# Retention and a bilinear FFN on one core: the last output product in two halves on two PSUM banks, and two products of h moved from GpSimd to VectorE

## Chip, core and metric

The kernel runs on one core of one Trainium2 chip. The metric is the device time of a run in microseconds (us). Times of the profile are those of one profiled execution of the same program.

## What is computed

A retention recurrence feeds a feed-forward block whose two input products are multiplied elementwise. Inputs and output are float32; products run in bfloat16 with float32 sums.

```
q, k, v: [4, 8, 768, 64]; w_a, w_b: [512, 1536]; w_out: [1536, 512]
state_t = gamma_h * state_{t-1} + k_t^T v_t        # per batch and head
y_t     = (1/8) * q_t state_t
x       = y, heads side by side: [3072, 512]
out     = ((x @ w_a) * (x @ w_b)) @ w_out          # [3072, 512]
```

## The kernel before, in words

The 3072 tokens are cut into 24 tiles of 128, in seven blocks `J` of 4, 2, 2, 2, 2, 4 and 8 tiles. Retention, the casts of weights and inputs, and the feed-forward blocks of earlier tokens are interleaved by hand: a helper `seq` chains every instruction to the one before it on its engine, so the order on each engine is the order of the text. Tiles come from pools with a fixed number of buffers; a new tile waits until the last reader of the buffer that it gets is done.

The last block (`BIG`, J = 6, 1024 tokens) is a stage of its own, run by `big()`. It replaces eight block products by seven with sums around them, twice.

The products with `w_a` and `w_b` are done by twelve units `u0` to `u11`. Unit `u` has a pair number `p = u // 2` and one of the weights, `a` for even and `b` for odd units. Its seven products (methods p1 to p7) go into three PSUM banks: "A" from a ring of three banks (`psff`), "B" from two fixed banks, one for the even and one for the odd units (`uB`), and "C". Each product is two matmuls of 512 columns. Bank A is built up in steps, and ScalarE copies it out after a step (`snap`, line 795). `Unit.leave` (line 797) adds a copy and a bank on VectorE: for an `a` unit into a tile `asb` (pool of 5 buffers), for a `b` unit into `gsb` (pool of 6). Behind a `gsb` stands the product of h = gsb * asb, 128x512 in bf16, on GpSimd for the pairs 0 to 4 and on VectorE for the last pair. That product is also the last reader of its `gsb` and `asb`. GpSimd works through sums of weights (`weight_pieces`, tiles `wsa` and `wsb`) in between.

The products with `w_out` are done by four groups `a`, `b`, `c`, `d` of 256 tokens (class `Group`), again seven products of 6 matmuls of 256 columns each, in banks `mA`, `mB`, `mC`. ScalarE copies bank A after steps 1, 6 and 5 into `snaps[:, 0]` to `snaps[:, 2]` (line 657). VectorE adds a copy to bank B or C into an output row tile `osb` (pool of 6 buffers), ScalarE copies bank A after the last step (p3), and `leave` (line 669) issues the output on SyncE's queue (SP).

The two orders `START` and `END` are written out by hand. The program closes with `c7 d7 c6 d6 S14 c5 d5 c3 c4 d4 d3`. So `d3`, the step p3 of group d, is the last product: six matmuls add S4 times the lower right quarter of `w_out` (`B22`) to bank A, ScalarE copies the 128x256 result (line 700), and two DMAs, one on ScalarE's queue and one on SP's, each send the rows of 64 partitions (line 702). Step `d4` stands directly ahead of it, with its own add on VectorE and its own output DMA on SP.

Of the kernel before, what the change touches and what calls it, by code (L numbers as in the profile page):

```python
# [9 lines left out]
F32 = mybir.dt.float32  # L10
BF16 = mybir.dt.bfloat16
AF = mybir.ActivationFunctionType
ALU = mybir.AluOpType
# [16 lines left out]
def kernel(  # L30
# [10 lines left out]
    nc = tc.nc  # L41
    P = 128
# [26 lines left out]
    osbp = ctx.enter_context(tc.tile_pool(name="osbp", bufs=6))  # L69
# [25 lines left out]
    psff = Ring()  # L95
# [4 lines left out]
    def seq(bi):  # L100
        ins = bi.ins
        prev = last.get(ins.engine)
        if prev is not None:
            tc.add_manual_dep(ins, prev.name, nosync, reason="program order")
        last[ins.engine] = ins
        return bi
# [125 lines left out]
    NP = NFT // 2  # L232
    DH = DM // 2
    wsum = wpool.tile([P, 3, NP, DH], BF16, name="wsum")
    wo_v = wo_bf.rearrange("p (two j) (c d) -> p two c j d", two=2, c=2)
    B11, B12, B21, B22 = (wo_v[:, k2, c] for k2 in range(2) for c in range(2))
    T2, T3, T4 = (wsum[:, n] for n in range(3))
    BIG = len(TILES) - 1
# [86 lines left out]
    def half(i):  # L325
        return slice(64 * i, 64 * i + 64)
# [63 lines left out]
    def leave(t):  # L390
        J, i = where[t]
        key, i = (J, i) if J < BIG else ((J, i // 4), i % 4)
        if i == 0:
            pool, tag = (wstage, "w") if key == (BIG, 1) else (xtp, "xt")
            xt[key] = pool.tile([P, KT, 4 * P], BF16, tag=tag, name="xt")
        for r in range(2):
            seq(nc.scalar.copy(xt[key][:, 2 * r : 2 * r + 2, i * P : (i + 2) * P],
                               ys[t // 2][r].rearrange("p j a s n -> p j (a s n)")))

    def turn(new, old, eng=nc.scalar):  # L400
        if old is not None:
            ys[old // 2] = [psat.tile([P, 2, 2, 2, P // 2], F32, tag=f"y{r}", name="y") for r in range(2)]
        two = new is not None and (new + 1) % NCH < NCH - 1
        if new is not None:
            if two or old is None:
                update(new, eng)
            scores(new + 1, "y" if old is None else "ff")
            scores(new, "at")
        if old is not None:
            inter(old)  # L410
            inter(old + 1)
        if two:
            update(new + 1, nc.scalar)
        elif new is not None and old is not None:
            update(new, eng)
        if old is not None:
            intra(old)
            intra(old + 1)
            leave(old)
# [158 lines left out]
    def rows(J, u, r):  # L578
        n0 = (sum(TILES[:J]) + 2 * u) * P
        return out[n0 : n0 + 2 * P, :].rearrange("(n r) d -> r n d", r=2)[r]  # L580

    def tt(dst, x, y, op, eng=nc.vector):
        seq(eng.tensor_tensor(dst, x, y, op=op))  # L583
# [13 lines left out]
    hs = {}  # L597
# [30 lines left out]
    class Group:  # L628
# [66 lines left out]
                self.leave(1, DH, DM)  # L695

        def p3(self):
            self.product("A", 4, B22, False)
            if self.J == BIG and self.i == 3:
                seq(nc.scalar.copy(self.row(0)[:, DH:], self.bank["A"]))  # L700
                for n, queue in enumerate((nc.scalar, nc.sync)):
                    seq(queue.dma_start(out=rows(self.J, self.i, 0)[half(n), DH:],
                                        in_=self.osb[0][half(n), DH:]))
                return
            seq(nc.scalar.copy(self.row(0)[:, DH:], self.bank["A"]))
            psff.back(self.whole["A"])
            self.leave(0)

        def p4(self):
            self.product("B", (1, 1), T4, False)  # L710
            tt(self.row(1)[:, :DH], self.bank["B"], self.snaps[:, 1], ALU.add)
            psff.back(self.whole["B"])
            self.leave(1, 0, DH if self.J == BIG and self.i > 1 else DM)
# [31 lines left out]
    def weight_pieces(n):  # L745
        for _ in range(min(n, len(pieces))):
            weight_piece(*pieces.pop(0))
# [16 lines left out]
    def h_big(c):  # L764
        if (BIG, c) not in ht:
            ht[BIG, c] = htp.tile([P, NFT, 4 * P], BF16, tag="ht", name="ht")
        return ht[BIG, c]

    class Unit:
# [27 lines left out]
        def leave(self, i, c, bank, n):  # L797
            if self.w == "a":
                dst = half_a[self.p, i, c] = asbp.tile([P, 4 * P], BF16, tag="asb", name="asb")
                tt(dst, self.bank[bank], self.snaps[n], ALU.add)  # L800
                return
            g = nat.tile([P, 4 * P], BF16, tag="vb", name="gsb")
            tt(g, self.bank[bank], self.snaps[n], ALU.add)
            tt(h_big(c)[:, NP * i + self.p], g, half_a.pop((self.p, i, c)), ALU.mult,
               nc.gpsimd if self.p < NP - 1 else nc.vector)
            weight_pieces(2 if self.p < 2 else 1)

        def p1(self):
# [270 lines left out]
```

## Time and profile before

| what | value |
|---|---|
| median of 3 runs | 221.32 us (220.12 to 221.72) |
| the profiled execution | 220.11 us |
| its span from first to last instruction | 218.4 us (218.402) |
| granted TensorE clock | 0.999 |
| TensorE busy | 211.5 us, 97% of the span |
| GpSimd busy | 150.0 us, 69% |
| VectorE busy | 139.5 us, 64% |
| ScalarE busy | 100.9 us, 46% |

In the lines of the profile, PE is TensorE's matmul, PEld its weight load, DVE VectorE, ACT ScalarE, POOL GpSimd, SPq and ACTq the DMA issues on the queues of SyncE and ScalarE. L583 is line 583 of the kernel, here a helper `tt` that all two-input adds and products go through, so tiles tell them apart and not the line. A timeline row has the start in us, the length, engine, line, operation, output<-inputs with partitions x elements and types, and a count; in brackets stands the engine's idle time ahead of it and who ended it. The length of a row with several matmuls runs to the end of the last, which overlaps the next one's start.

### The profile page before, as it was taken

The page shows a single profiled execution, that of the slowest core. Times are in us where ns is not written, and L with a number is a line of the kernel's source. Part 1 is how long each engine was busy: PE and PEld are TensorE (multiplying, and loading weights), DVE is VectorE, ACT ScalarE, POOL GpSimd, SP SyncE. Part 2 cuts the span into 40 slices and gives each one's busy share as a digit, 9 for nine tenths or more (in the row PEclk, how much of TensorE's full clock was granted, in tenths as well). Part 3 has the DMA queues.
Part 4 walks back from the last instruction along what each step waited for, and adds up shares of the span by engine and source line. Part 5 has one row for each costly group of instructions (what it writes and reads, how often), then busy time and mean ns, then how long its engine had stood idle before and what let it go on. Part 6 is the DMA issues. An engine that isn't in the chain of part 4 may idle for free.

```text
span 218.4 us, 5659 instructions
## 1 busy us (share of the span) xinstructions
PE 211.5 (97%) x2238; PEld 143.5 (66%) x2238; DVE 139.5 (64%) x255; ACT 100.9 (46%) x221; POOL 150.0 (69%) x174
## 2 busy tenths in 40 slices
PE   7889999999999999999999999999999999999993
PEld 3557445687458888888888655457864444458882
DVE  3776346845883485455477246876678676788961
ACT  3256335343234445464576245456545665652430
POOL 5265876878444578569847949989999999970000
PEclk9999999999999999999999999999999999999999
DMA  6999999999999999999999999970022000000145
GB/s 164 290 322 366 384 310 358 384 253 240 183 255 246 200 230 217 194 218 245 211 177 254 209 209 230 246 80 5 3 88 104 0 2 3 0 2 0 36 183 168
DMA packets 85018, 39.68 MB, mean 182 GB/s; under 512 B 57472, under 2 KB 78720, under 8 KB 84992
## 3 DMA queue, kind: packets, MB, share of 16 engines
q1 hardware_dynamic: 84912, 39.26, 79.8%
q8 instruction: 17, 0.28, 0.6%
q10 hardware_dynamic: 80, 0.07, 0.1%
q14 instruction: 9, 0.07, 0.1%
HBM read 28.31 MB, written 6.29 MB: 158 GB/s over the span
## 4 chain that ended last, share of the span: by engine, by line
PE 89%; SPq 4%; DMA 4%; POOL 0%; issue 0%; ACT 0%
PE g L545 19%; PE a L533 19%; PE mA L650 12%; PE uA L788 9%; PE mB L650 6%; PE uB L788 5%; PE o L570 5%; DMA wstb<-in_moe_w_b_dram 4%; SPq L132 3%; PE mC L650 3%; PE at L338 2%; PE uC L788 2%; PE y L386 2%; PE st L356 2%; PE y L376 1%; SPq L152 1%
## 5 line engine op out<-in xcount | busy, mean ns | idle before, releaser
L547 DVE TENSOR_TENSOR ht<-g,asb 128x256 bf16<-128x256 f32 (+1 forms) x74 | 37.2, 503 | 37.8 <-PE g L545 34.4
L533 PE MATMUL a<-xt,wa_bf 128*128 128x256 bf16 (+1 forms) x296 | 52.7, 305 | 0.1
L545 PE MATMUL g<-xt,wb_bf 128*128 128x256 bf16 (+1 forms) x296 | 52.5, 304 | 0.2 <-POOL wb_bf L244 0.2
L536 ACT CAST asb<-a 128x256 bf16<-128x256 f32 (+1 forms) x74 | 32.3, 437 | 39.1 <-PE a L533 36.0
L545 PEld LDWEIGHTS <-wb_bf 128*128 128x128 bf16 x296 | 28.6, 98 | 12.7 <-POOL wb_bf L244 0.3
L533 PEld LDWEIGHTS <-wa_bf 128*128 128x128 bf16 x296 | 28.0, 98 | 12.2 <-POOL wa_bf L244 0.4
L285 POOL TENSOR_TENSOR kqb<-kf,ktab 128x512 bf16<-128x512 f32 x22 | 22.8, 1042 | 15.1 <-DMA kf<-in_k_dram 9.4
L795 ACT COPY snap<-uA 128x512 f32<-128x512 f32 x36 | 20.0, 588 | 15.5 <-PE uA L788 15.5
L650 PEld LDWEIGHTS <-hs 128*128 128x128 bf16 x240 | 23.4, 98 | 4.1
L285 POOL TENSOR_TENSOR kqb<-qf,qtab 128x512 bf16<-128x512 f32 x18 | 19.4, 1079 | 8.3 <-DMA qf<-in_q_dram 8.3
L344 DVE TENSOR_TENSOR aT<-at,mask 128x512 bf16<-128x512 f32 x36 | 22.3, 682 | 0.3
L657 ACT COPY snaps<-mA 128x256 f32<-128x256 f32 x30 | 11.0, 374 | 20.1 <-PE mA L650 20.1
L650 PEld LDWEIGHTS <-ht 128*128 128x128 bf16 x180 | 17.5, 98 | 3.2
L583 POOL TENSOR_TENSOR hs<-ht,hs 128x384 bf16<-128x384 bf16 (+1 forms) x17 | 16.7, 987 | 2.5 <-DVE ht L547 2.5
L583 POOL TENSOR_TENSOR ht<-gsb,asb 128x512 bf16<-128x512 bf16 x15 | 17.2, 1158 | 0.0
L583 POOL TENSOR_TENSOR hs<-ht 128x384 bf16<-128x384 bf16 (+2 forms) x12 | 13.8, 1152 | 3.2 <-DVE ht L547 3.2
L650 PE MATMUL mA<-wsum,hs 128*128 128x256 bf16 x120 | 15.2, 273 | 0.0
L244 POOL CAST vb<-vf 128x512 bf16<-128x512 f32 x16 | 10.1, 643 | 7.0 <-DMA vf<-in_v_dram 6.8
L583 DVE TENSOR_TENSOR osb<-mB,snaps 128x256 f32<-128x256 f32 x20 | 8.4, 422 | 8.4 <-PE mB L650 4.2
L583 DVE TENSOR_TENSOR asb<-uB,snap 128x512 bf16<-128x512 f32 x12 | 8.2, 685 | 4.5 <-POOL ht L583 2.4
L570 PE MATMUL o<-wo_bf,ht 128*128 128x512 bf16 x48 | 10.7, 379 | 0.0
L583 DVE TENSOR_TENSOR gsb<-uB,snap 128x512 bf16<-128x512 f32 x12 | 8.2, 687 | 3.6 <-ACT snap L795 1.8
(97 smaller groups left out, 332.1 us busy)
## 6 DMA issues: line engine op xcount, KB each, us to landing
qf<-in_q_dram SPq DMA_DIRECT2D x12, 512.0 KB, 6.6
out_dram<-osb SPq DMA_DIRECT2D x21, 256.0 KB, 4.0
kf<-in_k_dram SPq DMA_DIRECT2D x18, 256.0 KB, 4.7
vf<-in_v_dram SPq DMA_DIRECT2D x18, 256.0 KB, 5.2
wsta<-in_moe_w_a_dram SPq DMA_DIRECT2D x6, 512.0 KB, 7.9
wstb<-in_moe_w_b_dram SPq DMA_DIRECT2D x6, 512.0 KB, 8.2
wsto<-in_moe_w_out_dram SPq DMA_DIRECT2D x6, 512.0 KB, 8.7
kf<-in_k_dram SPq DMA_DIRECT2D x3, 512.0 KB, 7.1
```

What stands on the lines that cost most here:

```text
L285: seq(eng.tensor_tensor(dst, src, tab, op=ALU.mult))
L344: seq(nc.vector.tensor_tensor(aT[t][:, r], at[r], mask.to_broadcast([P, HP, P]), op=ALU.mult))
L533: seq(nc.tensor.matmul(a, wa_bf[:, kt, fs], xcols(J, kt, c0, c1), start=(kt == 0), stop=(kt == KT - 1)))
L536: seq(nc.scalar.copy(asb, a))
L545: seq(nc.tensor.matmul(g, wb_bf[:, kt, fs], xcols(J, kt, c0, c1), start=(kt == 0), stop=(kt == KT - 1)))
L547: seq(nc.vector.tensor_tensor(ht[J][:, ft, c0:c1], g, asbs.pop((J, ft, c0)), op=ALU.mult))
L570: seq(nc.tensor.matmul(o, ht[J][:, ft, i * P : (i + 1) * P], wo_bf[:, ft], start=(ft == 0), stop=(ft == NFT - 1), skip_group_check=True))
L583: seq(eng.tensor_tensor(dst, x, y, op=op))
L650: seq(nc.tensor.matmul(m, w, right[:, j], start=(first and j == 0), stop=(j == NP - 1), skip_group_check=True))
L657: seq(nc.scalar.copy(self.snaps[:, n], self.bank["A"]))
L788: seq(nc.tensor.matmul(m, w, right[:, k], start=(first and k == 0), stop=(k == 1), skip_group_check=True))
L795: seq(nc.scalar.copy(self.snaps[n], self.bank["A"]))
```

## The change

The first part concerns `d3`. Group d's p3 now calls `last_two`. It takes a second bank, `rest`, from the ring. The six matmuls of 256 columns become twelve of 128 columns: six add the first 128 columns to bank A as before, and six compute the second 128 columns from zero in `rest`, so the same weights are loaded twice. ScalarE copies the first half out of bank A and issues its DMA. VectorE adds `rest` and `snaps[:, 2]` (bank A as copied before this product) for the second half, and SP issues that DMA. Each half has an `osb` tile of its own, of 128x128, and each DMA sends 128 partitions of 512 bytes in place of 64 partitions of 1024.

The second part moves two of the fifteen products of h on GpSimd to VectorE: those of bank "C" of pairs 1 and 2, in the units `u3` and `u5`.

```diff
         def p3(self):
+            if self.J == BIG and self.i == 3:
+                self.last_two()
+                return
             self.product("A", 4, B22, False)
-            if self.J == BIG and self.i == 3:
-                seq(nc.scalar.copy(self.row(0)[:, DH:], self.bank["A"]))
-                for n, queue in enumerate((nc.scalar, nc.sync)):
-                    seq(queue.dma_start(out=rows(self.J, self.i, 0)[half(n), DH:],
-                                        in_=self.osb[0][half(n), DH:]))
-                return
             seq(nc.scalar.copy(self.row(0)[:, DH:], self.bank["A"]))
             psff.back(self.whole["A"])
             self.leave(0)
+
+        def last_two(self):
+            rest = psff.tile([P, 4 * P], F32, tag="ff", name="rest")
+            for n, bank in enumerate((self.bank["A"], rest)):
+                c = slice(n * P, (n + 1) * P)
+                for j in range(NP):
+                    seq(nc.tensor.matmul(bank[:, c], hs[self.key, 4][:, j, self.n], B22[:, j, c],
+                                         start=(n == 1 and j == 0), stop=(j == NP - 1),
+                                         skip_group_check=True))
+                osb = osbp.tile([P, P], F32, tag="osb", name="osb")
+                if n == 0:
+                    seq(nc.scalar.copy(osb, bank[:, c]))
+                else:
+                    tt(osb, bank[:, c], self.snaps[:, 2, c], ALU.add)
+                seq((nc.scalar, nc.sync)[n].dma_start(
+                    out=rows(self.J, self.i, 0)[:, DH + n * P : DH + (n + 1) * P], in_=osb))
...
             tt(h_big(c)[:, NP * i + self.p], g, half_a.pop((self.p, i, c)), ALU.mult,
-               nc.gpsimd if self.p < NP - 1 else nc.vector)
+               nc.vector if self.p == NP - 1 or (self.p, bank) in ((1, "C"), (2, "C")) else nc.gpsimd)
             weight_pieces(2 if self.p < 2 else 1)
```

## The prediction

> **What bounds the kernel now.** I read the page first (busy times, then the chain that ended last), then the time windows of the last block, then the timelines of single engines around the two edited places.
>
> ```profile
> span 218.4 us, 5659 instructions
> ...
> PE 211.5 (97%) x2238; PEld 143.5 (66%) x2238; DVE 139.5 (64%) x255; ACT 100.9 (46%) x221; POOL 150.0 (69%) x174
> ...
> PE 89%; SPq 4%; DMA 4%; POOL 0%; issue 0%; ACT 0%
> ```
>
> TensorE is busy for 97% of the span and carries 89% of the chain, and GpSimd and VectorE carry none of it. So an edit can move the end in two ways: it closes or opens a gap in TensorE's stream, or it changes what stands between TensorE's last product and the last byte written. One window holds the stage of the second edit (columns: length, PE, PEld, DVE, ACT, POOL busy, granted clock, DMA share, GB/s):
>
> ```profile
> 163.00:194.00 31.00, 31.00 (x145) 13.99 (x144) 22.22 (x35) 19.66 (x37) 30.69 (x32) 1.00 0.07 26
> ```
>
> From 163 to 194 GpSimd is full, 30.69 of 31.00 us, and VectorE is not, 22.22. TensorE looks full too, but its pipelined records hide short stalls, so I read its starts. Products of two 512-column matmuls start 0.43 us apart (181.69, 182.12), except once:
>
> ```profile
> 181.69 0.59 PE L788 MATMUL uA<-xt,wa_bf 128*128 128x512 bf16 x2
> 182.12 0.59 PE L788 MATMUL uA<-xs,wsb 128*128 128x512 bf16 x2
> 182.71 0.59 PE L788 MATMUL uB<-xs,wsb 128*128 128x512 bf16 x2
> ...
> 180.18 1.15 POOL L583 TENSOR_TENSOR ht<-gsb,asb 128x512 bf16<-128x512 bf16 x1
> ...
> 181.37 0.69 DVE L583 TENSOR_TENSOR asb<-uB,snap 128x512 bf16<-128x512 f32 x1 [1.45 <-POOL ht L583]
> 181.98 0.68 DVE L583 TENSOR_TENSOR gsb<-uB,snap 128x512 bf16<-128x512 f32 x1
> ...
> 179.25 0.68 DVE L583 TENSOR_TENSOR asb<-uC,snap 128x512 bf16<-128x512 f32 x1
> ...
> 179.53 0.59 PE L788 MATMUL uB<-xs,wsa 128*128 128x512 bf16 x2
> ```
>
> The product at 182.71 should have started at 182.12 + 0.43 = 182.55: a stall of 0.16 us. It writes the odd units' bank uB, whose last reader is the VectorE add at 181.98, which ends at 182.66. That add was late because the one ahead of it waited 1.45 us for an asb buffer, which the GpSimd product from 180.18 to 181.33 held. In the timeline every other start from 163 to the last matmul follows its forerunner at its own spacing (0.43 us for such a product, 0.11 for a matmul of 256 columns), so this is the only stall there.
>
> The end itself:
>
> ```profile
> 213.80 0.82 PE L650 MATMUL mA<-wo_bf,hs 128*128 128x256 bf16 x6
> ...
> 214.00 0.42 DVE L583 TENSOR_TENSOR osb<-mB,snaps 128x256 f32<-128x256 f32 x1 [0.23 <-PE mB L650]
> 214.65 0.37 ACT L700 COPY osb<-mA 128x256 f32<-128x256 f32 x1 [1.59 <-PE mA L650]
> ...
> 214.45 0.33 SPq L669 DMA_DIRECT2D out_dram<-osb  x1
> 215.05 0.56 SPq L702 DMA_DIRECT2D out_dram<-osb  x1
> 215.05 0.58 ACTq L702 DMA_DIRECT2D out_dram<-osb  x1
> ...
> out_dram<-osb SPq DMA_DIRECT2D x1, 64.0 KB, 2.1
> out_dram<-osb ACTq DMA_DIRECT2D x1, 64.0 KB, 2.3
> ```
>
> The last six matmuls run from 213.80 to 214.62, ScalarE copies until 215.02, and both DMAs are issued at 215.05. SP's lands 2.1 us later, ScalarE's 2.3 us later, at 217.35. From there to the end of the span (218.40) stand 1.05 us of closing waits, which no edit touches.
>
> **Part two first, the products of h.** Two instructions leave GpSimd and come to VectorE:
>
> ```profile
> L583 POOL TENSOR_TENSOR ht<-gsb,asb x15: 1151/1155/1168, 164.1 to 194.1; 128x512 bf16<-128x512 bf16 x15
> L583 DVE TENSOR_TENSOR ht<-gsb,asb x3: 424/425/661, 194.9 to 199.5; 128x512 bf16<-128x512 bf16 x3
> ...
> 169.81 0.69 DVE L583 TENSOR_TENSOR gsb<-uC,snap 128x512 bf16<-128x512 f32 x1 [0.44 <-PE uC L788]
> 171.40 0.69 DVE L583 TENSOR_TENSOR gsb<-uB,snap 128x512 bf16<-128x512 f32 x1 [0.90 <-ACT snap L795]
> ...
> 175.85 0.69 DVE L583 TENSOR_TENSOR gsb<-uC,snap 128x512 bf16<-128x512 f32 x1
> 177.44 0.69 DVE L583 TENSOR_TENSOR gsb<-uB,snap 128x512 bf16<-128x512 f32 x1 [0.90 <-ACT snap L795]
> ```
>
> GpSimd loses 2 x 1.155 us. VectorE gains 2 x 0.43 to 0.66 us (0.66 is the one of its three that ran beside GpSimd; I take 0.66). The two products come right behind the uC adds at 169.81 and 175.85, and both times VectorE then idles 0.90 us for ScalarE's copy. They fit, and their inputs were both written by VectorE, so they wait for nobody and nothing queues behind a wait. If the cover were gone, the second would make VectorE 0.66 us late. Its adds up to the one at 179.25 would end at 180.59 and not at 179.93, the two late adds would start at 180.59 and 181.20, and the bank would be free at 181.88, still ahead of 182.55: no cost.
>
> On GpSimd, what follows u3's removed product moves up by 1.155 us at most; of the two, only this one stands ahead of 180.18. The asb buffer then comes free near 180.2 and not at 181.33. The VectorE add needs its own product too (started 179.53, over at 180.12), so it starts near 180.25, and the bank is free at about 181.5. TensorE then starts at 182.55. Gain 0.16 us. The gain is all or nothing: the buffer has to come 0.16 us earlier, and anything beyond that is wasted. What could eat it is contention. Beside a VectorE sum of two SBUF tensors, a GpSimd sum takes 1.60 us, and 1.15 without:
>
> ```profile
> 154.53 1.60 POOL L583 TENSOR_TENSOR wsa<-wa_bf,wsa 128x512 bf16<-128x512 bf16 x1
> ...
> 155.21 1.47 DVE L583 TENSOR_TENSOR xs<-xs,xt 128x1024 bf16<-128x1024 bf16 x1
> ```
>
> Two such stretches (0.45 each) leave 0.25 us of the shift, still over 0.16. The Trainium skill ("GPSIMD Engine Reference", Key points) says that the engine shares its SBUF interfaces with VectorE, contended by instructions with two SBUF inputs, which is what the moved products are; the row agrees, and by the rule too the term stays 0.16. Bounds 0 and 0.16. With the stall gone nothing on TensorE is late next: none of its other starts waits for VectorE or GpSimd.
>
> **Part one, the last product.** It removes six matmuls of 256 columns, one ScalarE copy, and two DMAs of 64 rows. It adds twelve matmuls of 128 columns with their weight loads, a ScalarE copy of 128 columns, a VectorE add of 128 columns, and two DMAs of 128 rows of 512 B. No DMA is added, and no queue is passed. All in the clock of before, without the 0.16:
>
> ```profile
> 33.90 0.61 PE L442 MATMUL tp<-ident,kqb 128*128 128x128 bf16 x8
> ...
> 40.49 0.61 PE L485 MATMUL y<-kqT,gbd 128*128 128x128 bf16 x8
> ...
> L485 PEld LDWEIGHTS <-gbd 128*128 128x128 bf16 x20 | 1.2, 98 | 0.4
> ```
>
> Eight 128-column matmuls, each with its own full weight load, take 0.61 us, the last alone 0.22: (0.61 - 0.22) / 7 = 0.056 us apart. So the first half ends at 213.80 + 5 x 0.056 + 0.22 = 214.30 and the second at 213.80 + 11 x 0.056 + 0.22 = 214.64, against 214.62 before. Loading the weights twice is hidden under the matmuls at this spacing. The upper bound is 0.098 us apart, if a load (98 ns) were not hidden at all: second half at 215.10.
>
> The Trainium skill ("TensorE: Matmul & The Clock Gate", Back-to-back issue gap) speaks against this edit: it gives about 81 ns per matmul for a stream of load and matmul pairs at 128 columns, and 56 only for matmuls alone. By it the second half would end 11 x 0.025 = 0.28 us later, an estimate from that page, and the time below would be 221.03. The rows above are such pairs and show 56.
>
> ```profile
> L795 ACT COPY snap<-uA 128x512 f32<-128x512 f32 x36 | 20.0, 588 | 15.5 <-PE uA L788 15.5
> L657 ACT COPY snaps<-mA 128x256 f32<-128x256 f32 x30 | 11.0, 374 | 20.1 <-PE mA L650 20.1
> L583 DVE TENSOR_TENSOR osb<-mB,snaps 128x256 f32<-128x256 f32 x20 | 8.4, 422 | 8.4 <-PE mB L650 4.2
> L583 DVE TENSOR_TENSOR asb<-uB,snap 128x512 bf16<-128x512 f32 x12 | 8.2, 685 | 4.5 <-POOL ht L583 2.4
> ...
> L669 SPq DMA_DIRECT2D out_dram<-osb x1: 332/332/332, 214.4 to 214.4; - x1
> ...
> DMA to landing us min/median/max: 1.9/1.9/1.9
> ```
>
> No row has 128 columns on these engines. Going on from 512 to 256 to 128 by the same steps gives the copy 0.26 us (bounds 0 and 0.37) and the add 0.29 (0 and 0.42). The copy runs 214.33 to 214.59, and ScalarE's DMA is issued at 214.62. Even with 2.3 us it lands by 216.92. The add runs 214.67 to 214.96; VectorE is free since 214.42, SP since 214.78 (the d4 issue at 214.45), so the last DMA is issued at 214.99.
>
> Its landing: the d4 DMA, 128 rows of 1024 B issued alone, took 1.9 us with an issue of 0.33. The two of L702, issued together, took 2.1 and 2.3 with issues of 0.56 and 0.58, though each has half the rows and bytes. Issuing apart is what the edit buys. No row has 512 B to DRAM; as many rows of half the size should take no longer than 1.9, and a collision as before 2.3. The two issues still overlap a little, so I take 1.95: it lands at 216.94, against 217.35. Gain 0.41 us (bounds 0.06 with 2.3 us and 0.46 with 1.9; the bounds of the add move it by 0.13 down or 0.29 up).
>
> **The sum.** 0.16 + 0.41 = 0.57 us. Span 218.40 - 0.57 = 217.83; outside it the profiled execution has 220.11 - 218.40 = 1.71 us, so the profiled execution would come to 219.54. It was the lowest of the runs shown, 1.21 below the median. On the median, 221.32 - 0.57 = 220.75 us.
>
> **Rivals.** First, weight loads at 98 ns: the last DMA moves back by 0.46, the tail gain becomes -0.05, and 0.11 us are left: 221.21 us. For it: a load is longer than a 56 ns slot. Against it: the rows of L442 and L485.
>
> Second, part two doesn't do what it says: TensorE keeps its 0.16 us, because GpSimd is stretched by more than computed or the stall moves to another bank. Then 220.91 us. For it: the gain hangs on one wait of 1.45 us. Against it: only 0.16 of the up to 1.15 us is needed.
>
> Third, and on the other side: the new osb tiles wait for a buffer. The halves no longer use a tile that group d already owns but take two new ones from a pool of six, with three tiles of c and d still on their way out. If the first got the buffer of c4, whose DMA is issued at 213.79, the copy would wait for its landing.
>
> ```profile
> 213.79 0.99 SPq L669 DMA_DIRECT2D out_dram<-osb  x2
> ...
> DMA to landing us min/median/max: 2.2/2.2/2.2
> ...
> 208.53 4.68 SPq L669 DMA_DIRECT2D out_dram<-osb  x3
> ```
>
> That is 215.99; copy, issue and 2.3 us bring the landing to 218.62, 1.27 us after today's; less the 0.16 of part two, 1.11 us are lost, and the time is 222.4 us. It makes the kernel slower as soon as the copy starts after 214.9. For it: the pool is small. Against it: a's and b's last DMA was issued at 208.53, which leaves buffers that have been free for about three us by 214.
>
> **How the numbers follow.** The forecast (both gains) has 0.64, weight loads 0.08, no gain in part two 0.12, the buffer wait 0.09, and something not seen here 0.07. Alone the forecast's cases lie within 0.3 us of 220.75. The runs before spread by -1.20 and +0.40 about their median, more than all bounds together, and the range has to hold that: 219.5 at the low end (220.75 - 1.2) and 222.0 at the high end, between the forecast with a high run (221.2) and the buffer wait (222.4). About 1% is what a measurement of this kernel can tell from no change; every case here is below it. Faster by over 1% would need more than TensorE's one stall and the whole shortening of the tail: 0.05, for the spread of the runs. Slower by over 1%: 0.08, most of it the unseen and part of the buffer wait. Within 1%: 0.87.
>
> **What would show it.** Right: TensorE's products follow each other at 0.43 us past 182 with no gap; no VectorE wait of 1.45 us on GpSimd; two more ht<-gsb,asb rows on VectorE, 13 on GpSimd; twelve matmuls of 128x128 at the end, 0.056 us apart; the ScalarE copy at about 0.5 us after the first of them; an issue of the last DMA alone on SP about 1.2 us after the first matmul; landing about 1.95 us after that. Wrong: a spacing near 0.08 or 0.1, an idle time ahead of the last copy put down to a DMA, a landing of 2.3 us for the last DMA, or a span over 218.4.

## The result, and the profile after

The changed kernel takes 219.57 us (median of 9 runs, 219.34 to 219.97), the kernel before 220.41 us in the same comparison (9 runs, 220.00 to 221.72). The ratio is 0.9958, with a 95% interval of 0.9938 to 0.9978: 0.2% to 0.6% faster, which is clear of noise and well under 1%. The 221.32 us that the prediction started from was the median of three runs, two of them high; 35 later runs of the kernel before have a median of 220.3.

The profile's page after the change, and the window of the products of h:

```profile
span 217.9 us, 5672 instructions
...
PE 211.4 (97%) x2244; PEld 143.6 (66%) x2244; DVE 141.5 (65%) x258; ACT 100.8 (46%) x221; POOL 147.9 (68%) x172
...
163.00:194.00 31.00, 31.00 (x145) 14.01 (x143) 23.81 (x38) 19.64 (x37) 29.83 (x30) 1.00 0.07 25
```

Work moved as written: GpSimd lost 2.1 us, VectorE gained 2.0. The span is 0.51 us shorter (218.40 to 217.89). Next the timelines of the end, and the landing of the last two DMAs (lines 711 to 719 lie in the new `last_two`):

```profile
213.93 0.50 PE L711 MATMUL mA<-wo_bf,hs 128*128 128x128 bf16 x6
...
214.26 0.50 PE L711 MATMUL rest<-wo_bf,hs 128*128 128x128 bf16 x6
214.51 0.27 ACT L716 COPY osb<-mA 128x128 f32<-128x128 f32 x1 [1.32 <-PE mA L711]
214.80 0.29 DVE L583 TENSOR_TENSOR osb<-rest,snaps 128x128 f32<-128x128 f32 x1 [0.24 <-PE rest L711]
214.80 0.37 ACTq L719 DMA_DIRECT2D out_dram<-osb  x1
215.12 0.33 SPq L719 DMA_DIRECT2D out_dram<-osb  x1
...
out_dram<-osb ACTq DMA_DIRECT2D x1, 64.0 KB, 1.9
out_dram<-osb SPq DMA_DIRECT2D x1, 64.0 KB, 1.8
```

The last landing is at 215.12 + 1.80 = 216.92, which is 2.99 us after the first of the last matmuls; before it was 217.35 - 213.80 = 3.56. That is 0.57 us, and the closing waits shrank from 1.05 to 0.97 us besides.

And TensorE near 182 us, with the two engines behind its stall:

```profile
182.28 0.59 PE L801 MATMUL uA<-xs,wsb 128*128 128x512 bf16 x2
182.84 0.38 PE L801 MATMUL uB<-xs,wsb 128*128 128x512 bf16 x1
...
180.31 1.15 POOL L583 TENSOR_TENSOR ht<-gsb,asb 128x512 bf16<-128x512 bf16 x1
...
181.50 0.69 DVE L583 TENSOR_TENSOR asb<-uB,snap 128x512 bf16<-128x512 f32 x1 [1.14 <-POOL ht L583]
```

The stall is still there: 182.84 - 182.28 - 0.43 = 0.13 us, against 0.16 before (0.133 and 0.156 in the records). So the 0.51 us of the two profiles add up like this: 0.15 us longer up to the first product of the last block (150.95 against 150.80), 0.02 from the stall, 0.57 from the end, 0.08 from the closing waits. In these two executions the moved products gave next to nothing. In other executions they gave more, as the experiments show.

### The profile page after: what moved, and what is told of

It is laid out like the page before. It is cut to its first block, busy times and chain, and to the rows that moved or that the text cites. A ratio compares the mean times of both kernels' runs of the same rounds, so it can differ in the third digit from the quotient of the medians.

```text
span 217.9 us, 5672 instructions
## 1 busy us (share of the span) xinstructions
PE 211.4 (97%) x2244; PEld 143.6 (66%) x2244; DVE 141.5 (65%) x258; ACT 100.8 (46%) x221; POOL 147.9 (68%) x172
## 4 chain that ended last, share of the span: by engine, by line
PE 84%; SPq 7%; DMA 6%; issue 1%; POOL 0%; ACT 0%; DVE 0%; ACTq 0%
PE g L545 17%; PE a L533 17%; PE mA L650 11%; PE uA L801 10%; PE mB L650 6%; PE uB L801 5%; PE o L570 5%; SPq L132 4%; DMA wstb<-in_moe_w_b_dram 4%; PE mC L650 3%; DMA kqT<-kqb 2%; PE uC L801 2%; PE at L338 2%; PE y L386 2%; PE st L356 1%; PE y L376 1%
## 5 line engine op out<-in xcount | busy, mean ns | idle before, releaser
L650 PEld LDWEIGHTS <-hs 128*128 128x128 bf16 x234 | 22.8, 98 | 4.0
L583 POOL TENSOR_TENSOR ht<-gsb,asb 128x512 bf16<-128x512 bf16 x13 | 15.1, 1173 | 1.1 <-DVE gsb L583 1.1
L397 ACT CAST xt<-y 128x512 bf16<-128x512 f32 x18 | 9.7, 589 | 0.6 <-PE y L386 0.4
```

Source lines behind the costliest of these rows:

```text
L650: seq(nc.tensor.matmul(m, w, right[:, j], start=(first and j == 0), stop=(j == NP - 1), skip_group_check=True))
```

## The experiments

Kernels in one comparison share the runs of the kernel before, whose medians were 220.32 us in the first (35 runs) and 220.28 in the second (35 runs). The other kernels have 12 runs each. A ratio need not be the quotient of two medians: the kernel before has a long upper end of runs, and the quotient of the means lies nearer to the ratios that are given here.

**One part at a time.** First the last product alone:

```diff
-               nc.vector if self.p == NP - 1 or (self.p, bank) in ((1, "C"), (2, "C")) else nc.gpsimd)
+               nc.gpsimd if self.p < NP - 1 else nc.vector)
```

> The last product in two halves alone, products of h as before. Theory: the tail is nearly the whole gain. From the first of the twelve last matmuls to the last landing 2.99 us as in the changed kernel, against 3.56 before, so 0.55 us faster (ratio 0.9975); TensorE's stall near 182 us is between 0 and 0.8 us, as late as GpSimd happens to be. Rival: the tail carries less than half, and the rest of the measured 0.4% comes from the products of h; then the ratio is above 0.998.

Measured: 219.62 us, ratio 0.9965 (0.9942 to 0.9989). Its profile has 2.96 us from the first of the last matmuls to the last landing. The median is 0.70 us lower, in line with 0.57 plus the shorter closing waits. The interval alone would not exclude the rival's 0.998; the profile's 2.96 us does. The profiled execution was a late one, 220.35 us, and shows where such a run loses most of its time:

```profile
165.00 1.16 POOL L583 TENSOR_TENSOR ht<-gsb,asb 128x512 bf16<-128x512 bf16 x1
...
182.27 0.69 DVE L583 TENSOR_TENSOR asb<-uB,snap 128x512 bf16<-128x512 f32 x1 [1.79 <-POOL ht L583]
...
182.49 0.59 PE L801 MATMUL uA<-xs,wsb 128*128 128x512 bf16 x2
183.61 0.59 PE L801 MATMUL uB<-xs,wsb 128*128 128x512 bf16 x2 [0.53 <-DVE gsb L583]
```

GpSimd's first product of h starts at 165.00 and not at 164.11, and the stall is 183.61 - 182.49 - 0.43 = 0.69 us. The block itself began later too, at 151.16 and not at 150.80.

Then the moved products alone:

```diff
-               nc.gpsimd if self.p < NP - 1 else nc.vector)
+               nc.vector if self.p == NP - 1 or (self.p, bank) in ((1, "C"), (2, "C")) else nc.gpsimd)
```

> The two products of h on VectorE alone, last product as before. Theory: worth 0.0 to 0.2 us (ratio 0.999 to 1.000), because in the changed kernel the stall near 182 us was still 0.13 us: GpSimd came into the stage 0.6 us later (a late load of k) and was stretched by 0.47 us beside the two moved products, which together ate the 1.15 us saved. Rival: most runs of the kernel before have a larger stall than its profile, and the move takes 0.3 to 0.6 us off them: ratio 0.997 to 0.9985.

Measured: 220.06 us (219.88 to 220.33), ratio 0.9972 (0.9954 to 0.9991). That is the rival's range, and the theory's touches the interval only at its edge. The profile still has a stall of 0.14 us:

```profile
182.17 0.60 PE L788 MATMUL uA<-xs,wsb 128*128 128x512 bf16 x2
182.74 0.59 PE L788 MATMUL uB<-xs,wsb 128*128 128x512 bf16 x2
```

Yet the move is worth 0.26 us in the median and 0.47 in the mean (220.09 against 220.56), and above all it cuts off the upper end: 15 of the 35 runs of the kernel before are over 220.45 us, none of these 12. The two parts alone add up to more than the whole change (0.70 + 0.26 = 0.96 us in medians against 0.84), which the intervals allow.

**How late GpSimd is.** The kernel before, unchanged:

> The kernel before, unchanged, for the noise of the ratio and for a second look at how late GpSimd is. Ratio 1.000 within 0.002. If GpSimd's lateness is a matter of when loads land, its first product of h starts somewhere between 164.1 and 165 us, and TensorE's stall near 182 us is 0.16 us plus whatever GpSimd is later than in the first profile; if it is fixed by the program, both are as in the first profile (164.1 and 0.16).

Measured: 220.36 us, ratio 0.9989 (0.9968 to 1.0010), 6 of 12 runs over 220.45. In its profile GpSimd's first product of h starts at 164.18, the stall is 0.19 us. That is nearly the first profile again, so this run alone does not show that the lateness varies; the profiles of the other kernels, whose code is the same up to there, do. Then GpSimd was made late, by a sum of weights that is done twice ahead of its first product of h:

```diff
+    pieces.insert(8, ("a", 3, 1, 2))
...
-    weight_pieces(8)
+    weight_pieces(9)
     big()
```

> The kernel before with one more GpSimd instruction ahead of the block, a sum of weights of 128x256 that is done twice (0.62 us); nothing else. Theory: GpSimd has no idle time between there and 182 us, so its lateness goes through to TensorE one to one: the stall near 182 us is 0.6 us larger than without for the same lateness, and the median rises by 0.5 to 0.65 us, ratio 1.0025. Rival: the stall near 182 us is TensorE's own or hangs on VectorE alone; then nothing moves (ratio 1.000).

Measured: 221.24 us, ratio 1.0039 (1.0018 to 1.0060), 0.96 us above the kernel before for an instruction of 0.62 us. GpSimd's and TensorE's records of it:

```profile
164.86 1.14 POOL L583 TENSOR_TENSOR ht<-gsb,asb 128x512 bf16<-128x512 bf16 x1
...
182.22 0.59 PE L789 MATMUL uA<-xs,wsb 128*128 128x512 bf16 x2
183.47 0.59 PE L789 MATMUL uB<-xs,wsb 128*128 128x512 bf16 x2 [0.66 <-DVE gsb L583]
```

The stall is 0.82 us. The theory of a one-to-one passage holds for the profile (0.66 us more than in the first profile, for a GpSimd that is 0.66 later in the block); the median moved by somewhat more, which this run does not explain. The same edit in the changed kernel:

> The changed kernel with the same extra GpSimd instruction of 0.62 us. Theory: the two moved products give a margin of about 0.65 us, so part of the lateness is absorbed: where GpSimd comes early the stall is 0.1 us, where it comes late 0.7 us; the median rises by 0.2 to 0.6 us above the changed kernel's 219.57, and the loss is smaller than that of the same instruction in the kernel before. Rival: no margin was gained (the moved products only changed where VectorE waits); then the loss is the same 0.6 us as there.

Measured: 220.11 us, ratio to before 0.9972 (0.9949 to 0.9995): 0.54 us above the changed kernel, against 0.96 above the kernel before. By the times alone this is weak, since the rival expected 0.6. The profile shows the margin:

```profile
182.23 0.59 PE L802 MATMUL uA<-xs,wsb 128*128 128x512 bf16 x2
183.23 0.59 PE L802 MATMUL uB<-xs,wsb 128*128 128x512 bf16 x2 [0.40 <-DVE gsb L583]
```

The stall is 0.57 us, with GpSimd later than in the kernel before made late, where it is 0.82. The table has every profile in which TensorE stalls at this place. The lateness is taken from the block's first product on TensorE (uA) to GpSimd's first product of h:

| kernel | uA | first ht on GpSimd | lateness | stall near 182 us |
|---|---|---|---|---|
| one DMA (below) | 150.77 | 164.09 | 13.32 | 0.16 |
| before | 150.80 | 164.11 | 13.31 | 0.16 |
| before, again | 150.83 | 164.18 | 13.35 | 0.19 |
| last product alone | 151.16 | 165.00 | 13.84 | 0.69 |
| before, made late | 150.89 | 164.86 | 13.97 | 0.82 |
| changed | 150.95 | 164.88 | 13.93 | 0.13 |
| moved products alone | 150.84 | 164.79 | 13.95 | 0.14 |
| changed, made late | 150.90 | 165.49 | 14.59 | 0.57 |

With all fifteen products on GpSimd the stall is the lateness less 13.15 us, within 0.01. With two moved, what has to be taken off is 13.80 us (14.02 in the last row). So the moved products buy 0.65 to 0.87 us of lateness. An execution that is 13.32 late gets its 0.16 us back, one that is 13.95 late gets 0.65.

The rows of GpSimd say where these two figures come from. A product of h holds its place in the queue for 1.11 us, from its start to the next one's start:

```profile
164.88 1.16 POOL L583 TENSOR_TENSOR ht<-gsb,asb 128x512 bf16<-128x512 bf16 x1
165.99 1.16 POOL L583 TENSOR_TENSOR wsa<-wa_bf 128x512 bf16<-128x512 bf16 x1
```

One removed product ahead of the wait is worth that, less what the moved products stretch GpSimd by: 0.47 us in the changed kernel (shown further down), 0.25 in the changed kernel made late. That leaves 0.64 and 0.86 us.

Not all of the spread between executions is this stall. The block's first product on TensorE starts between 150.77 and 151.16 us in the table, and in the next experiment at 151.60.

**Is it the buffer?** The kernel before with one more asb buffer:

```diff
-    asbp = ctx.enter_context(tc.tile_pool(name="asbp", bufs=5))
+    asbp = ctx.enter_context(tc.tile_pool(name="asbp", bufs=6))
```

> The kernel before with six buffers for asb in place of five, nothing else: the wait of VectorE for the buffer that a GpSimd product holds goes away without moving a product. Theory: the stall near 182 us is that wait and nothing else, so it is gone in the profile, and TensorE has no late start from 163 us to the last matmul; time 0.1 to 0.2 us lower (ratio 0.9990 to 0.9995). Rival: the stall moves to the next wait on GpSimd (the gsb buffers), and the time stays (ratio 1.000).

Measured: 220.45 us, ratio 1.0006 (0.9984 to 1.0028). The interval holds the theory's ratio as well as the rival's, so the time does not decide between them; the profile does. The profiled execution was a late one again (lateness 14.20, which would make a stall of 1.05 us near 182), and there the stall is gone. TensorE stops elsewhere:

```profile
183.02 0.59 PE L788 MATMUL uA<-xs,wsb 128*128 128x512 bf16 x2
183.45 0.60 PE L788 MATMUL uB<-xs,wsb 128*128 128x512 bf16 x2
...
186.04 0.59 PE L788 MATMUL uA<-xs,wsa 128*128 128x512 bf16 x2
186.91 0.59 PE L788 MATMUL uB<-xs,wsa 128*128 128x512 bf16 x2 [0.27 <-DVE asb L583]
...
200.00 0.81 PE L650 MATMUL mB<-wsum,hs 128*128 128x256 bf16 x6 [0.39 <-DVE asb L583]
```

The product at 186.91 is 186.91 - 186.04 - 0.43 = 0.44 us late, and TensorE idles another 0.39 us ahead of 200.00. So the wait near 182 was for that buffer, but what costs is GpSimd's backlog: here the sixth buffer passed most of it on to later waits.

**The end.** The kernel before with one DMA in place of two:

```diff
-                for n, queue in enumerate((nc.scalar, nc.sync)):
-                    seq(queue.dma_start(out=rows(self.J, self.i, 0)[half(n), DH:],
-                                        in_=self.osb[0][half(n), DH:]))
+                seq(nc.sync.dma_start(out=rows(self.J, self.i, 0)[:, DH:], in_=self.osb[0][:, DH:]))
```

> The kernel before with its last output sent by one DMA of 128 rows of 1024 B on SP, in place of two of 64 rows on two queues at once; last product and copy as before. Theory: most of what the tail gained is that two DMAs issued at the same moment slow each other (issues of 0.56 and 0.58 us, landings 2.1 and 2.3 us after issue). One alone issues in 0.33 and lands 1.9 us after issue, so from the first of the last matmuls to the last landing 3.13 us in place of 3.56, 0.43 us faster: ratio 0.998. Rival: the gain comes from the first half leaving earlier and from the shorter rows; then one DMA lands about as late as two, 3.5 us, ratio 0.9995 to 1.000.

Measured: 220.03 us, ratio 0.9975 (0.9955 to 0.9994). Its profile:

```profile
213.78 0.82 PE L650 MATMUL mA<-wo_bf,hs 128*128 128x256 bf16 x6
...
214.63 0.37 ACT L700 COPY osb<-mA 128x256 f32<-128x256 f32 x1 [1.59 <-PE mA L650]
215.03 0.33 SPq L701 DMA_DIRECT2D out_dram<-osb  x1
...
DMA to landing us min/median/max: 1.9/1.9/1.9
```

The issue takes 0.33 us and not 0.56, and the landing comes 3.11 us after the first of the last matmuls, 0.45 us earlier than with two. So in the profiles 0.45 of the 0.57 us are to be had by merging the two DMAs, with the last product left as it was, and cutting the product in two adds the other 0.12. The median is only 0.25 us lower.

**A third product moved**, in the changed kernel:

```diff
-               nc.vector if self.p == NP - 1 or (self.p, bank) in ((1, "C"), (2, "C")) else nc.gpsimd)
+               nc.vector if self.p == NP - 1 or (self.p, bank) in ((0, "C"), (1, "C"), (2, "C")) else nc.gpsimd)
```

> The changed kernel with a third product of h on VectorE, that of bank C of pair 0. Theory: TensorE's stall near 182 us is GpSimd's backlog beyond a margin (0.16 at 13.31 us from the block's first product to GpSimd's first product of h, 0.69 at 13.84; with two products moved 0.13 at 13.93). A third move adds 0.6 to 1.1 us of margin, so the profile shows no stall near 182 us, and the time is 0.0 to 0.15 us below the changed kernel's 219.57 (ratio to before 0.995 to 0.996). Rival: VectorE, busy with its own sums near 160 us, is late with the moved product and puts a new stall on TensorE there: 0.3 us or more above the changed kernel.

Measured: 219.49 us (219.25 to 219.99), ratio to before 0.9960 (0.9943 to 0.9977). There is no stall near 182 any more:

```profile
182.04 0.59 PE L801 MATMUL uA<-xs,wsb 128*128 128x512 bf16 x2
182.47 0.59 PE L801 MATMUL uB<-xs,wsb 128*128 128x512 bf16 x2
...
L583 DVE TENSOR_TENSOR ht<-gsb,asb x6: 424/537/1011, 160.1 to 199.2; 128x512 bf16<-128x512 bf16 x6
```

The theory holds for the stall, and the rival's new stall near 160 us is not there. The 0.08 us by which the median is below the changed kernel's is within the intervals of both, so this is not shown to be faster.

## Why the prediction was right or wrong, point by point

Two steps failed: the one from the spread of three runs to what a measurement can tell, and in part two the price of the stall.

**The direction and the sum.** It forecast 0.57 us less and put 0.87 on a time within 1%, on the ground that about 1% is what a measurement can tell from no change. That step failed. The time did stay within 1%, but the interval of the ratio is 0.4% wide and lies wholly below 1: a change of 0.84 us in the median was told from none. The base was off as well: 221.32 us, the median of three runs, is 0.91 above the 220.41 of nine, so the forecast of 220.75 us was 1.18 too high, although its step of 0.57 us, a ratio of 0.9974, lies within the measured interval. The gain in the two profiles, 0.51 us, was near the forecast by luck. The end gave 0.24 us more than forecast (0.57 + 0.08 against 0.41); the stall gave 0.14 less, and the block began 0.15 later.

**Part one, the matmuls.** Right: twelve matmuls 0.056 us apart (the second six start 0.33 us after the first), all weight loads hidden. Neither the 98 ns bound nor the 81 ns of the Trainium skill's page "TensorE: Matmul & The Clock Gate" (Back-to-back issue gap) showed: by an estimate from that page's 81 ns, the second six would have started 0.49 us after the first.

**Part one, copy and add.** Right: 0.27 and 0.29 us, against 0.26 and 0.29 taken from 512 and 256 columns.

**Part one, the landing.** Mis-sized: 1.95 us were taken, 1.80 came, for rows of 512 B, with nothing else being issued on SP. This makes the tail 0.57 us and not 0.41. The closing waits, counted as untouched, gave 0.08 more. The prediction said that issuing apart is what the edit buys. The single DMA shows that 0.45 us hang on sending two halves of 64 rows at one moment. Whether it is the moment or the 64 rows was not tried separately; two queues alone are not the cost, since the changed kernel uses two and its issues take 0.37 and 0.33 us.

**Part two, the 0.16 us.** This is the step of the mechanism that failed. "The gain is all or nothing" took the stall of one profile for a fixed quantity. It is not: it is GpSimd's lateness less 13.15 us, and the lateness differs between profiled executions of the same GpSimd program by 0.5 us and more (13.31 to 13.84 in the table, 14.20 with the sixth buffer). The profiled execution of before happened to be an early one. In the changed kernel's, GpSimd was 0.62 us later, the moved products stretched it by 0.47 us (0.28 and 0.19 in the rows of 1.43 and 1.34 us below, against 1.15 us each undisturbed), and 1.09 of the 1.11 us saved were used up. The 0.02 left are the 0.02 that the stall shrank by. The prediction had allowed 0.45 us for each of two stretches; their sum was about half of that, and what it had put at nothing was GpSimd's own lateness.

```profile
170.69 1.43 POOL L583 TENSOR_TENSOR wsb<-wb_bf,wsb 128x512 bf16<-128x512 bf16 x1
...
176.54 1.15 POOL L583 TENSOR_TENSOR wsb<-wb_bf,wsb 128x512 bf16<-128x512 bf16 x1
177.65 1.34 POOL L583 TENSOR_TENSOR ht<-gsb,asb 128x512 bf16<-128x512 bf16 x1
...
170.69 0.43 DVE L583 TENSOR_TENSOR ht<-gsb,asb 128x512 bf16<-128x512 bf16 x1
...
176.73 1.24 DVE L583 TENSOR_TENSOR ht<-gsb,asb 128x512 bf16<-128x512 bf16 x1
177.89 0.68 DVE L583 TENSOR_TENSOR gsb<-uB,snap 128x512 bf16<-128x512 f32 x1
```

The second rival, that TensorE keeps its stall, described this profile. But its price, no gain from part two, was wrong for the runs: the move alone is worth 0.26 us in the median, and more where GpSimd is late.

**Cover and price of the moved products.** VectorE's idle time held the first (0.43 us) and not quite the second: 1.24 us against 0.66 taken and 0.90 idle, so the add after it (the last row above) started at 177.89. Before it started at 177.44; less the 0.15 us by which the whole block was later, that is 0.30 us late. As the prediction had worked out for a VectorE late by up to 0.66 us, that cost TensorE nothing.

**The buffer wait.** It did not come: the last ScalarE copy waited for TensorE alone (1.32 us in the timeline).

**Why GpSimd is late in one execution and not in another** is only read, not tried: between 112 and 146 us it waits for loads of k, q and v, and then runs without a gap into the block, so that what it loses there it cannot make up.

```profile
POOL kqb L285 <- DMA qf<-in_q_dram: 2.3, 2, 1.6
POOL kqb L285 <- DMA kf<-in_k_dram: 2.0, 1, 2.0
...
POOL kqb L285 <- DMA kf<-in_k_dram: 3.8, 2, 3.1
POOL kqb L285 <- DMA qf<-in_q_dram: 0.8, 1, 0.8
POOL vb L244 <- DMA vf<-in_v_dram: 0.5, 1, 0.5
```

The first two rows are of the kernel before, the other three of the changed kernel (total, times, longest wait). They add up to 4.3 and 5.1 us (GpSimd's waits for VectorE in the same window are 3.8 us in both), and the difference is about the 0.77 us by which GpSimd's first product of h came later (164.88 against 164.11). What makes a load land later stays open.

## What to carry to other kernels

A stall behind a queue that has no idle time need not be a fixed number; here it was 0.16 us in one execution and 0.69 in another. So find the point where that queue last waited, take the lateness from there, and cost an edit over the range of lateness, not at the one profile's value. Such an edit can show nothing in a pair of profiles and still be worth something wherever that engine is later. At a kernel's end, look at how the last DMAs are issued before cutting the last product: here two halves issued at the same moment landed 0.45 us later than one whole.

## What the runs showed of the hardware that was not expected

Two DMAs of 64 rows issued within 0.01 us on the queues of SP and ScalarE took 0.56 and 0.58 us to issue and landed 2.1 and 2.3 us later. One of 128 rows with the same bytes took 0.33 and 1.9. Issued 0.32 us apart, ScalarE's took 0.37 and 1.9 us and SP's 0.33 and 1.8.

A product of two bf16 tiles of 128x512 in SBUF took VectorE between 0.42 and 1.24 us, and which it was depended on who started first. Where a sum or product on GpSimd was under way, VectorE's product ended 0.28 to 0.29 us after that instruction's end, however early it had started: in the rows above it started at 176.73, beside the sum from 176.54 to 177.69, and ended at 177.97. All 17 such rows of the ten profiles do so. Where both started at 170.69, VectorE's took its 0.43 us and GpSimd's sum 1.43 in place of 1.15.
